# A longer row in the MLP's on-chip tiles: activations 450 instead of 448 columns apart, weights' tiles 898 instead of 896 columns

## The chip, the core and the metric

The kernel runs on one core of a Trainium2 chip. Its engines work side by side, each through its own list of instructions: PE (TensorE, matrix products; its weight loads are shown apart as PEld), DVE (VectorE), ACT (ScalarE), POOL (GpSimd) and SP, which issues most of the DMAs. They meet at semaphores. On-chip memory (SBUF) has 128 partitions, and a tile takes the same byte range in each of them; matrix products land in a second memory, PSUM.

The metric is the time of one execution on the device, in microseconds. Traces come from executions with the hardware profiler on. Times of instructions are in nanoseconds where so marked.

## What is computed

The reference is one block with two residual branches on x of 2048 tokens by 448 channels, each behind a layer norm that is scaled, shifted and gated by a condition vector c. The first branch is a state-space convolution over the tokens, computed in the kernel through hand-made Fourier tables. The second is a small network across the tokens:

```python
x = A_u
mod = (_silu(c) @ w_mod).reshape(c.shape[0], 6, 1, -1)
sa, ca, ga, sb, cb, gb = (mod[:, 0], mod[:, 1], mod[:, 2], mod[:, 3], mod[:, 4], mod[:, 5])
h = _layernorm(x, axis=-1) * (1 + ca) + sa
x = x + ga * _A_ref(h, ...)                      # convolution along the tokens
h = _layernorm(x, axis=-1) * (1 + cb) + sb
x = x + gb * _B_ref(h, B_w1, B_b1, B_w2, B_b2)   # MLP along the tokens

def _B_ref(x, w1, b1, w2, b2):                   # S = 2048 tokens, D = 448, F = 1792
    h = _layernorm(x, axis=-1)                   # (B, S, D)
    u = _gelu(jnp.einsum("bsd,sf->bdf", h, w1) + b1)
    y = jnp.einsum("bdf,fs->bds", u, w2) + b2
    return y.transpose(0, 2, 1)
```

The change touches the tiles of `_B_ref` alone.

## The kernel before

The convolution fills the first 400 us or so. The MLP comes last, and every product of it is made of three matmuls in the type fp32r, a rounded fp32. Each fp32 operand is split into a rounded high part and the remainder as a low part, and the kernel sums high x high, high x low and low x high.

*Activations.* `h3h` and `h3l` (lines 1320 and 1321) hold the high and low part of the normed tokens: 128 partitions, 16 rows of D = 448 columns of four bytes. Row r is the moving operand (`h3h[:, r]`) of the matmuls on lines 1332 to 1334. They are written by ACT (lines 1237 and 1243) and DVE (1240 and 1244), one row for each turn of the loop over t on line 1339. `uh` and `ul` hold the same for the hidden layer after the gelu, in two halves of 7 rows each (lines 1322, 1323, 1387 and 1388). DVE writes them row by row behind ACT's gelu (lines 1373 to 1375), and lines 1401 to 1403 read them.

*Weights.* `WeightStream` brings 64 tiles of 128 x 896. A DMA loads the raw fp32 tile `w` (lines 187 and 190), ACT rounds it into `whi` (line 207), and DVE writes what is left into `wlo` (line 216). `whi` and `wlo` have four buffers each (WAHEAD), `w` three. Each tile has seven slices of 128 columns, and each slice is a stationary operand, loaded into PE ahead of its matmul.

*Loops.* The first layer runs in two halves of seven hidden blocks. For each of the 16 rows r, `mlp1` takes one weight tile and does 7 x 3 matmuls into seven PSUM tiles `acc`. Then comes the gelu of the half. The second layer makes 16 output tiles `o`, each of 2 x 7 x 3 matmuls: kh picks the half of `uh` and `ul`, k the row. In all that is 2 x 16 x 21 + 16 x 42 = 1344 matmuls of 128 x 128 by 128 x 448, 224 on each of the six lines.

*Order.* PE, ACT, DVE and POOL do their work in the order in which the code issues it (`manual_schedule`). Weights are split up to four tiles ahead of use, on ACT and DVE, and a split has to wait until the matmuls have let a buffer go. During the first half, ACT and DVE also make the layer norm's rows (`ln_y`, `ln_mod`, `ln_out`) just ahead of the matmuls that read them. In the second half and the second layer they only split weights, apply the gelu and write outputs (lines 1405 to 1407).

*Other matmuls that the prediction speaks of.* Line 485 makes the modulation vectors in plain fp32: the moving operand is `wm` or, later, rows of `xt`, 448 columns each, and the stationary one is `scb`. Line 1212 belongs to the first two rows of the convolution's output and moves 224 columns against `fl`. Line 1202 makes the other rows.

Of the kernel before, what the change touches and what calls it, by code (L numbers as in the profile page):

```python
# [12 lines left out]
F32R = mybir.dt.float32r  # L13
# [8 lines left out]
L, D, N, F = 2048, 448, 256, 1792  # L22
P = 128
# [136 lines left out]
def token_pair(a, r, g):  # L160

    rows = a.rearrange("(n g h r) d -> g n h (r d)", g=2, h=2, r=16)
    return rows[g, :, :, r * D : (r + 2) * D]


class WeightStream:
# [32 lines left out]
    def begin(self, most):  # L199

        n = self.done
        if n >= min(most, 64):
            return None
        w = self.raw.pop(n)
        hi = self.pool.tile([P, 896], F32R, tag="whi", name="whi")
        lo = self.pool.tile([P, 896], F32R, tag="wlo", name="wlo")
        self.nc.scalar.copy(hi, w)  # L207
        self.parts[n] = hi, lo
        self.done += 1
        return w, hi, lo  # L210
# [11 lines left out]
def tile_adaln_s4d_mixer(ctx, tc, i, out):  # L222
# [20 lines left out]
    with ExitStack() as es:  # L243
# [796 lines left out]
        for s in range(tail):  # L1040
# [80 lines left out]
            if s == 16:  # L1121
                spec.close()
                up = early.enter_context(tc.tile_pool(name="up", bufs=3, reuse_waits="tile"))
# [43 lines left out]
        def ln_load(r, ahead=True):  # L1167
            vts[r] = rot.tile([P, 2, D], F32, tag="vt", name="vt", bufs=4)
            nc.sync.dma_start(vts[r], v_v[r])
            if ahead and r % 2 and 1 < r < 15:  # L1170
                x_pair(r + 1)
# [26 lines left out]
        def ln_y(r):  # L1198
            y = py.tile([P, D], F32, tag="y", name="y")
            vt = vts.pop(r)  # L1200
            for g in range(2):
                T.matmul(y[64 * g : 64 * g + 64], ft, vt[:, g], start=True, stop=True)  # L1202
            return y_sum(r, y)
# [16 lines left out]
        def ln_mod(r):  # L1220
            mean, rs = sa.pop(r)
            h = rot.tile([P, D], F32, tag="h", name="h", bufs=3)
            total = small("sum", "b")
            V.reciprocal(rs, rs)
            V.scalar_tensor_tensor(h, xts[r // 2][:, r % 2], mean, mod[4], ALU.add, ALU.mult)
            V.scalar_tensor_tensor(h, h, rs, mod[3], ALU.mult, ALU.add, accum_out=total)  # L1226
            sb[r] = stats(h, total, "b")
            hs[r] = h

        def ln_out(r):  # L1230
            mean, rs = sb.pop(r)
            h = hs.pop(r)
            V.reciprocal(rs, rs)
            V.tensor_tensor(mean, mean, rs, ALU.mult)
            if r == 0:

                S.activation(h3h[:, r], h, AF.Identity, bias=mean, scale=rs)  # L1237
                exact = rot.tile([P, D], F32, tag="h", name="h", bufs=3)
                V.tensor_scalar(exact, h, rs, mean, ALU.mult, ALU.add)
                V.tensor_tensor(h3l[:, r], exact, h3h[:, r].bitcast(F32), ALU.subtract)  # L1240
                return None
            S.activation(h, h, AF.Identity, bias=mean, scale=rs)  # L1242
            S.copy(h3h[:, r], h)
            return lambda: V.tensor_tensor(h3l[:, r], h, h3h[:, r].bitcast(F32), ALU.subtract)
# [69 lines left out]
    with ExitStack() as es:  # L1314
        es.enter_context(tc.manual_schedule(engines={ENG.PE, ENG.Activation, ENG.DVE, ENG.Pool}))
        V, S, G = nc.vector, nc.scalar, nc.gpsimd
        kp = es.enter_context(tc.tile_pool(name="mk", bufs=1))
        up = es.enter_context(tc.tile_pool(name="mu", bufs=1))
        pacc = es.enter_context(tc.tile_pool(name="pacc", bufs=7, space=PSUM))
        h3h = kp.tile([P, 16, D], F32R, name="h3h")  # L1320
        h3l = kp.tile([P, 16, D], F32R, name="h3l")
        uh = [up.tile([P, 7, D], F32R, name="uh0"), None]
        ul = [up.tile([P, 7, D], F32R, name="ul0"), None]

        def mlp1(acc, n, f0=0, f1=7):
            fh, r = divmod(n, 16)
            hi, lo = wst.parts[n]
            if f1 == 7:
                wst.parts.pop(n)
            for f in range(f0, f1):  # L1330
                fs = slice(f * P, (f + 1) * P)
                nc.tensor.matmul(acc[f], hi[:, fs], h3h[:, r], start=r == 0, stop=False)  # L1332
                nc.tensor.matmul(acc[f], hi[:, fs], h3l[:, r], start=False, stop=False)  # L1333
                nc.tensor.matmul(acc[f], lo[:, fs], h3h[:, r], start=False, stop=r == 15)  # L1334

        first = ExitStack()
        first.enter_context(tc.manual_schedule(engines={ENG.SP}))
        acc = [pacc.tile([P, D], F32, tag="acc", name="acc") for _ in range(7)]
        for t in range(-2, 16):

            part = wst.begin(t + WAHEAD - 1) if t > 0 else None
            last = ln_out(t + 1) if 0 <= t + 1 < 16 else None

            if t == -1:
                second()
            if t == 0:
                part = wst.begin(3)
                mlp1(acc, 0, 0, 4)
                ln_y(3)()
            if t == -1 or 0 < t < 13:  # L1350
                ln_y(t + 3)()
            if 4 <= t + 7 < 16:
                ln_load(t + 7)
            if t < 0:
                wst.load()
            if 1 <= t + 2 < 16:
                ln_mod(t + 2)
            if last:
                last()
            wst.rest(part, V)  # L1360
            if t == 0:
                mlp1(acc, 0, 4, 7)
            elif t > 0:
                mlp1(acc, t)
        first.close()
        e3.close()
        ru = es.enter_context(tc.tile_pool(name="m2r", bufs=3))

        def gelu(acc, fh):
            for f in range(7):  # L1370
                k = 7 * fh + f
                u = ru.tile([P, D], F32, tag="u", name="u")
                S.activation(u, acc[f], AF.Gelu_apprx_tanh, bias=b1[:, k : k + 1])
                V.tensor_copy(uh[fh][:, f], u)
                V.tensor_tensor(ul[fh][:, f], u, uh[fh][:, f].bitcast(F32), ALU.subtract)

        gelu(acc, 0)
        acc = [pacc.tile([P, D], F32, tag="acc", name="acc") for _ in range(7)]
        for r in range(16):
            if r < 8:  # L1380
                for g in range(2):
                    rows = xts[r][64 * g : 64 * g + 64].rearrange("p r d -> p (r d)")
                    nc.sync.dma_start(token_pair(x2_d, 2 * r, g), rows)
            wst.ahead(16 + r + WAHEAD, V)
            mlp1(acc, 16 + r)
        e2.close()
        uh[1] = up.tile([P, 7, D], F32R, name="uh1")
        ul[1] = up.tile([P, 7, D], F32R, name="ul1")
        gelu(acc, 1)
        for t in range(16):  # L1390
            ss = slice(t * P, (t + 1) * P)
            xt = ru.tile([P, D], F32, tag="x2", name="x2")
            nc.sync.dma_start(xt, x2_d[ss])
            o = pacc.tile([P, D], F32, tag="acc", name="o")
            for kh in range(2):
                n = 32 + 2 * t + kh
                wst.ahead(n + WAHEAD, V)
                hi, lo = wst.parts.pop(n)
                for k in range(7):
                    ks = slice(k * P, (k + 1) * P)  # L1400
                    nc.tensor.matmul(o, hi[:, ks], uh[kh][:, k], start=kh == 0 and k == 0, stop=False)  # L1401
                    nc.tensor.matmul(o, hi[:, ks], ul[kh][:, k], start=False, stop=False)  # L1402
                    nc.tensor.matmul(o, lo[:, ks], uh[kh][:, k], start=False, stop=kh == 1 and k == 6)  # L1403
            y = ru.tile([P, D], F32, tag="y", name="y")
            V.scalar_tensor_tensor(y, o, b2[:, t : t + 1], mod[5], ALU.add, ALU.mult)  # L1405
            V.tensor_tensor(y, y, xt, ALU.add)  # L1406
            nc.sync.dma_start(out[0, ss], y)
# [27 lines left out]
```

## Time and profile before

| | us |
|---|---|
| median of three runs | 698.45 (691.95, 698.45, 699.45) |
| profiled execution, its time | 695.37 |
| profiled execution, span from the first to the last instruction | 693.2 |
| PE busy in the span | 621.5 |
| first and last start of a matmul of the MLP | 403.4 and 688.5 |
| mean granted TensorE clock, as a share of full speed | 0.958 |

The prediction shows the lines. A row of a group reads: line, engine, operation, the tiles it writes and reads, how often, then durations. PE and PEld have rows of their own, because a weight load runs beside the matmul before it. The ends of matmuls in the trace are modelled, since they are pipelined; the distance from one start to the next is the better measure of what one costs. An "idle before" belongs to the engine, with the work whose end closed the wait.

### The profile page before, as it was taken

To read this page: it belongs to the slowest core of one execution; us is meant where nothing else is said; L and a number is where in the kernel's file an instruction comes from. 1 tells how busy PE (TensorE), PEld (TensorE's weight loads), DVE (VectorE), ACT (ScalarE), POOL (GpSimd) and SP (SyncE) were. 2 spreads that over 40 slices of the span, in tenths; PEclk is the share of its full clock that TensorE was granted. 3 is DMA by queue.
4 is the path that set the end of the run, shared out by engine and by line. 5 is a ranking of instruction groups with operands and counts; after the bars stand their busy time and mean duration, and the time that the engine had idled before them with its cause. 6 is when DMAs were issued, how large, how long until landed. Compare 5 with 4: busy or idle time off the path is not lost. (4 is left out here: it accounts for less than half of the span.)

```text
span 693.2 us, 18255 instructions
## 1 busy us (share of the span) xinstructions
PE 621.5 (90%) x7180; PEld 462.5 (67%) x7180; DVE 456.7 (66%) x880; ACT 437.6 (63%) x876; POOL 269.2 (39%) x323
## 2 busy tenths in 40 slices
PE   0878889889988779898899989999999999999997
PEld 0444445545535556565567757778999999999996
DVE  7578799879779468685877577776622354444431
ACT  5867599788977789999973578777422332222220
POOL 6497468259368768889766300000000000000000
PEclk9997979899999989899999999999999999999999
DMA  7694646567895526444248799965674445556540
GB/s 173 195 194 110 219 163 217 208 203 233 252 298 170 156 72 159 128 132 146 84 128 261 245 269 264 243 152 149 168 242 112 141 132 160 160 159 170 167 129 27
DMA packets 104275, 121.14 MB, mean 175 GB/s; under 512 B 12858, under 2 KB 92254, under 8 KB 104062
## 3 DMA queue, kind: packets, MB, share of 16 engines
q1 hardware_dynamic: 102830, 113.92, 56.8%
q0 software_dynamic: 1360, 6.06, 4.1%
q8 instruction: 57, 0.93, 0.6%
q14 instruction: 28, 0.23, 0.1%
HBM read 84.59 MB, written 34.87 MB: 172 GB/s over the span
## 5 line engine op out<-in xcount | busy, mean ns | idle before, releaser
L207 ACT CAST whi<-w 128x896 fp32r<-128x896 f32 x64 | 59.7, 938 | 131.7 <-PE o L1402 84.6
L650 POOL TENSOR_TENSOR G<-mag,gs 128x512 f32<-128x512 f32 x56 | 72.3, 1290 | 73.2 <-ACT gs L646 70.7
L216 DVE TENSOR_TENSOR wlo<-w,whi 128x896 fp32r<-128x896 f32 x64 | 68.0, 1086 | 40.3 <-ACT whi L207 31.0
L1332 PE MATMUL acc<-h3h,whi 128*128 128x448 f32 x224 | 83.3, 372 | 1.4 <-ACT h3h L1237 1.4
L681 PEld LDWEIGHTS kg<-E,G 128*32 128x32 f32 x3584 | 59.1, 118 | 36.5 <-issue 16.4
L1334 PE MATMUL acc<-h3h,wlo 128*128 128x448 f32 x224 | 82.0, 366 | 0.0
L1333 PE MATMUL acc<-h3l,whi 128*128 128x448 f32 x224 | 81.6, 364 | 0.2 <-DVE mean L1186 0.2
L1401 PE MATMUL o<-uh,whi 128*128 128x448 f32 x224 | 81.4, 363 | 0.0
L1403 PE MATMUL o<-uh,wlo 128*128 128x448 f32 x224 | 81.2, 363 | 0.0
L1402 PE MATMUL o<-ul,whi 128*128 128x448 f32 x224 | 80.7, 360 | 0.0
L598 PE MATMUL xg<-tab,lph 64*128 64x512 f32 x112 | 67.4, 604 | 11.6 <-DVE E L658 7.2
L681 PE MATMUL kg<-E,G 128*32 128x64 f32 x3584 | 69.4, 233 | 8.9 <-issue 4.1
L598 PE MATMUL xe<-tab,lph 64*128 64x512 f32 x112 | 66.9, 600 | 9.7 <-ACT gs L647 7.0
L651 POOL TENSOR_TENSOR G<-mag,gs 128x512 f32<-128x512 f32 x56 | 71.6, 1278 | 0.0
L1405 DVE SCALAR_TENSOR_TENSOR y<-o,b,mod 128x448 f32<-128x448 f32 x16 | 11.0, 685 | 80.2 <-PE o L1403 80.2
L627 POOL TENSOR_TENSOR m<-mag,w 128x512 f32<-128x512 f32 x56 | 59.7, 1066 | 4.6 <-POOL w L625 0.3
L652 DVE TENSOR_TENSOR E<-m,xe 128x512 f32<-128x512 f32 x56 | 38.0, 679 | 28.4 <-ACT xe L645 24.5
L1332 PEld LDWEIGHTS acc<-h3h,whi 128*128 128x128 f32 x224 | 42.5, 190 | 13.6 <-ACT h L1242 6.3
L598 PE MATMUL xe<-tab,lex 64*128 64x512 f32 x56 | 32.0, 584 | 18.4 <-POOL dsk L472 17.2
L635 ACT ACTIVATE ab<-xe 128x512 f32<-128x512 f32 x56 | 34.0, 607 | 20.4 <-PE xe L598 11.2
L609 ACT ACTIVATE mag<-xe 128x512 f32<-128x512 f32 x56 | 35.7, 637 | 15.1 <-PE xe L598 6.2
L1334 PEld LDWEIGHTS acc<-h3h,wlo 128*128 128x128 f32 x224 | 42.5, 190 | 3.3
(236 smaller groups left out, 1470.3 us busy)
## 6 DMA issues: line engine op xcount, KB each, us to landing
w<-in_B_w_dram SPq DMA_DIRECT2D x64, 224.0 KB
w<-in_B_w_dram SPq DMA_DIRECT2D x32, 448.0 KB
yu_d<-yt SPq DMA_DIRECT2D x16, 448.0 KB
yi<-yu_d SPq DMA_DIRECT2D x16, 448.0 KB
us_d<-uo SPq DMA_DIRECT2D x16, 448.0 KB
u<-us_d SPq DMA_DIRECT2D x32, 224.0 KB
v_d<-vt SPq DMA_DIRECT2D x32, 224.0 KB
vt<-v_d SPq DMA_DIRECT2D x14, 448.0 KB
```

The source lines that it names most:

```text
L207: self.nc.scalar.copy(hi, w)
L216: eng.tensor_tensor(lo, w, hi.bitcast(F32), ALU.subtract)
L598: T.matmul(out[k], lhs[r], rhs[r], start=start, stop=stop)
L650: G.tensor_tensor(Gt[:, 1], mg_, v32(sg), ALU.mult)
L651: G.tensor_tensor(Gt[:, 0], mg_, v32(cg_), ALU.mult)
L681: T.matmul(kgs[g][32 * q : 32 * q + 32, m], Gt[:, c, d], E[:, c, d], start=h == 0 and c == 0 and m == 0, stop=h == 1 and c == 1, skip_grou ...
L1332: nc.tensor.matmul(acc[f], hi[:, fs], h3h[:, r], start=r == 0, stop=False)
L1333: nc.tensor.matmul(acc[f], hi[:, fs], h3l[:, r], start=False, stop=False)
L1334: nc.tensor.matmul(acc[f], lo[:, fs], h3h[:, r], start=False, stop=r == 15)
L1401: nc.tensor.matmul(o, hi[:, ks], uh[kh][:, k], start=kh == 0 and k == 0, stop=False)
L1402: nc.tensor.matmul(o, hi[:, ks], ul[kh][:, k], start=False, stop=False)
L1403: nc.tensor.matmul(o, lo[:, ks], uh[kh][:, k], start=False, stop=kh == 1 and k == 6)
```

## The change

Five tiles get a row of two more columns, and the code goes on with a view that leaves these two columns out. The two columns are written and read by nothing. `h3h`, `h3l`, `uh` and `ul` get W = D + 2 = 450 columns a row, so rows are 1800 bytes apart instead of 1792. `whi` and `wlo`, which have one row to a partition, get 898 columns, 3592 bytes instead of 3584. The raw tile `w`, into which the DMAs write, stays as it is. A line is added at 1320 (`W = D + 2`), so all lines of the MLP behind it stand one further down in the changed kernel: the matmuls are on 1333 to 1335 and 1402 to 1404.

```diff
@@ class WeightStream, begin
-        hi = self.pool.tile([P, 896], F32R, tag="whi", name="whi")
-        lo = self.pool.tile([P, 896], F32R, tag="wlo", name="wlo")
+        hi = self.pool.tile([P, 898], F32R, tag="whi", name="whi")[:, 0:896]
+        lo = self.pool.tile([P, 898], F32R, tag="wlo", name="wlo")[:, 0:896]
         self.nc.scalar.copy(hi, w)
@@ the MLP's tiles
-        h3h = kp.tile([P, 16, D], F32R, name="h3h")
-        h3l = kp.tile([P, 16, D], F32R, name="h3l")
-        uh = [up.tile([P, 7, D], F32R, name="uh0"), None]
-        ul = [up.tile([P, 7, D], F32R, name="ul0"), None]
+        W = D + 2
+        h3h = kp.tile([P, 16, W], F32R, name="h3h")[:, :, 0:D]
+        h3l = kp.tile([P, 16, W], F32R, name="h3l")[:, :, 0:D]
+        uh = [up.tile([P, 7, W], F32R, name="uh0")[:, :, 0:D], None]
+        ul = [up.tile([P, 7, W], F32R, name="ul0")[:, :, 0:D], None]
@@ after the first layer
-        uh[1] = up.tile([P, 7, D], F32R, name="uh1")
-        ul[1] = up.tile([P, 7, D], F32R, name="ul1")
+        uh[1] = up.tile([P, 7, W], F32R, name="uh1")[:, :, 0:D]
+        ul[1] = up.tile([P, 7, W], F32R, name="ul1")[:, :, 0:D]
```

In the allocation of the built programs, `h3h` begins at byte 22304 of each partition in both kernels, and all six activation tiles begin 32 bytes past a multiple of 64. The weights' buffers were 3584 bytes apart, and are now 3616.

## The prediction

> **What bounds the kernel now.** I read the profile's page first (busy shares and chain), then busy time by stretch from the start of the MLP on, then the six matmul groups of the MLP with the smallest, middle and largest duration, then the timeline inside one stretch, and last what TensorE waited for.
>
> The profile's page has the span, the engines and the chain that ended last:
>
> ```profile
> span 693.2 us, 18255 instructions
> PE 621.5 (90%) x7180; PEld 462.5 (67%) x7180; DVE 456.7 (66%) x880; ACT 437.6 (63%) x876; POOL 269.2 (39%) x323
> ...
> PE acc L1332 7%; PE o L1401 7%; PE acc L1334 7%; PE acc L1333 7%; PE o L1403 6%; PE o L1402 6%; PE y L1202 2%; ACT whi L207 0%; ACT sq L1188 0%; ACT L1291 0%; ACT h3h L1237 0%; DVE h L1226 0%; DVE y L1405 0%; DVE h3l L1240 0%; DVE y L1406 0%
> ```
>
> All of the chain that the profile names at 6% and more is matmuls of the MLP, the instructions that read the tiles of the change. The stretches of the MLP, with busy time of PE, PEld, DVE, ACT, POOL, then clock, DMA share and GB/s:
>
> ```profile
> 420.00:440.00 20.00, 20.00 (x95) 15.08 (x94) 15.06 (x46) 16.32 (x36) 0.00 (x0) 1.00 1.06 259
> 440.00:460.00 20.00, 20.00 (x96) 15.08 (x95) 15.03 (x44) 15.99 (x35) 0.00 (x0) 1.00 0.95 213
> ...
> 480.00:554.00 74.00, 74.00 (x372) 69.39 (x371) 28.06 (x38) 23.38 (x30) 0.00 (x0) 1.00 0.60 171
> 554.00:693.20 139.20, 134.89 (x675) 126.14 (x673) 55.33 (x71) 29.67 (x33) 0.00 (x0) 1.00 0.48 138
> ```
>
> From 420 on PE has no idle time up to the last matmul. What PE waited for in the whole MLP (from 403 us) is two short waits at its start, 1.6 us together:
>
> ```profile
> PE acc L1332 <- ACT h3h L1237: 1.4, 1, 1.4
> PE acc L1333 <- DVE mean L1186: 0.2, 1, 0.2
> ```
>
> So the time from 403 us on is the number of MLP matmuls times their spacing. The groups that write `acc` and `o` (smallest, middle, largest duration in ns, then first and last start in us):
>
> ```profile
> L1332 PE MATMUL acc<-h3h,whi x224: 362/363/575, 403.4 to 553.7; 128*128 128x448 f32 x112
> L1333 PE MATMUL acc<-h3l,whi x224: 359/360/739, 404.1 to 553.9; 128*128 128x448 f32 x112
> L1334 PE MATMUL acc<-h3h,wlo x224: 360/363/576, 404.6 to 554.1; 128*128 128x448 f32 x112
> ...
> L1401 PEld LDWEIGHTS o<-uh,whi x224: 187/188/188, 554.1 to 687.9; 128*128 128x128 f32 x112
> L1401 PE MATMUL o<-uh,whi x224: 363/363/364, 554.3 to 688.1; 128*128 128x448 f32 x112
> ...
> L1402 PE MATMUL o<-ul,whi x224: 359/360/361, 554.5 to 688.3; 128*128 128x448 f32 x112
> ...
> L1403 PE MATMUL o<-uh,wlo x224: 362/363/368, 554.7 to 688.5; 128*128 128x448 f32 x112
> ```
>
> The 672 matmuls of the second half start from 554.3 to 688.5: 134.2 / 671 = 200.0 ns each. The timeline shows the same rhythm and the weight load beside it:
>
> ```profile
> 560.12 0.36 PE L1403 MATMUL o<-uh,wlo 128*128 128x448 f32 x1
> 560.12 0.19 PEld L1401 LDWEIGHTS o<-uh,whi 128*128 128x128 f32 x1
> 560.32 0.36 PE L1401 MATMUL o<-uh,whi 128*128 128x448 f32 x1
> 560.32 0.19 PEld L1402 LDWEIGHTS o<-ul,whi 128*128 128x128 f32 x1
> 560.52 0.36 PE L1402 MATMUL o<-ul,whi 128*128 128x448 f32 x1
> ```
>
> A load starts with the matmul before it, lasts 187 to 188 ns and ends 12 ns ahead of the next start. It is hidden; the 200 ns are the reading of 448 columns of a `h3h`, `h3l`, `uh` or `ul` row. All 1344 together are 1344 x 0.2 = 268.8 us of the 693.2. 1% of the time is 7.0 us, or 5.2 ns per MLP matmul, and about that much a measurement of this kernel can tell from no change.
>
> **The change, part by part.** The built program has the same instructions in the same order with the same waits, DMA issues included; only addresses differ. So no term comes from an added or moved instruction or a new wait, and each has to come from an instruction that lasts longer or shorter at its new place. In the allocation of the built programs `h3h` starts at byte 22304 of a partition, 32 past a multiple of 64, and `h3l`, `uh` and `ul` also stand at 32. Before, rows are 1792 bytes apart, a multiple of 64, and each row begins at 32 modulo 64. After, they are 1800 bytes apart and row r begins at 32 + 8r modulo 64.
>
> *Counts.* In the first half 14 of 16 rows leave the place 32, in the second 6 of 7: 672 x 14/16 + 672 x 6/7 = 588 + 576 = 1164 matmuls. Off every multiple of 32 are 12 of 16 and 5 of 7: 504 + 480 = 984. At 8 modulo 16 are 8 of 16 and 3 of 7: 336 + 288 = 624.
>
> *Moving operand (the only term on the path).* The trace of before has no matmul that reads a row at 8, 16 or 24 past a multiple of 32, so its price is bounded by the nearest rows. These are the plain fp32 matmuls, which stand as two records for each matmul of the program. L485 reads rows at 32 (`wm`) and rows at 0 modulo 64 (`xt`), and L1212 reads 224 columns at 32:
>
> ```profile
> L485 PEld LDWEIGHTS pm<-wm,scb x24: 186/190/337, 39.5 to 82.8; 112*128 112x128 f32 x24
> L485 PE MATMUL pm<-wm,scb x24: 538/539/1116, 39.5 to 83.2; 112*128 112x448 f32 x24
> ...
> L485 PE MATMUL pm<-xt,scb x24: 539/539/644, 109.8 to 146.9; 112*128 112x448 f32 x24
> L1212 PEld LDWEIGHTS y<-vt,fl x32: 186/190/191, 389.7 to 398.8; 128*128 128x128 f32 x32
> L1212 PE MATMUL y<-vt,fl x32: 352/353/458, 389.7 to 399.0; 128*128 128x224 f32 x32
> ```
>
> 539 against 539 ns: at those two places there is no difference. But they take (539 - 353) / 224 = 0.83 ns a column, and leave 353 - 224 x 0.83 = 167 ns that doesn't depend on columns. The MLP's fp32r matmul takes (363 - 167) / 448 = 0.44 ns a column, so it reads a row at about twice the rate, and may feel what L485 doesn't. At half of 0.83 it would last 353 ns; it lasts 363 with `h3h` or `uh` and 360 with `h3l` or `ul`, on average 9 ns more. These 9 ns are the only excess in the rows that a place could cause. Lower end: a row that leaves 32 loses all of it, 1164 x 9 = 10.5 us less. Upper end: a row off the multiples of 32 pays it once more, 984 x 9 = 8.9 us more. I take 0, from L485, whose pair of rows is the only like-for-like comparison of places.
>
> The Trainium skill (SBUF — State Buffer, Specifications) says that SBUF lines are 16 bytes and that each crossing to a new line pays a penalty, which speaks against this change. A row at 8 modulo 16 touches 113 such lines instead of 112; at an estimate of 1/112 of the 200 ns for the extra one, 624 matmuls would add 1.1 us, so by the rule the sum would be +1.1 us and by L485's rows 0. No row of before reads at such a place, so the trace can't decide between them, and both lie under what can be measured.
>
> *Weight loads.* `whi` and `wlo` tiles of 3592 bytes lie 3616 apart in their pool, so the tiles start at 32, 0, 32, 0 modulo 64, not at all places, and each slice of 128 columns keeps its tile's place. L485 loads `scb` at 0 and L1212 loads `fl` at 32: 190 ns both. Taken as 0; cover is the 12 ns ahead of the next matmul, and a load that grew by more would put the excess on the path of 1344 matmuls (5 ns over the cover is 6.7 us).
>
> *ACT and DVE.* The rows that write these tiles, over the MLP (count, busy us, mean ns, idle before and its releaser):
>
> ```profile
> L216 DVE TENSOR_TENSOR wlo<-w,whi 128x896 fp32r<-128x896 f32 x62 | 65.8, 1085 | 39.6 <-ACT whi L207 30.2 <-DMA w<-in_B_w_dram 9.3
> L207 ACT CAST whi<-w 128x896 fp32r<-128x896 f32 x62 | 57.9, 938 | 131.7 <-PE o L1402 84.6 <-PE acc L1333 38.5 <-DMA w<-in_B_w_dram 8.7
> ...
> L1375 DVE TENSOR_TENSOR ul<-u,uh 128x448 fp32r<-128x448 f32 x14 | 8.7, 625 | 0.5
> ...
> L1374 DVE CAST uh<-u 128x448 fp32r<-128x448 f32 x14 | 5.4, 387 | 6.0 <-ACT u L1373 6.0
> ```
>
> L207 mostly waits for PE to free a buffer: splits run ahead and are hidden as long as L216 stays under the 21 matmuls of a weight tile, 4.2 us, against 1.09. The one row that could lose a faster mode is L1374, which copies 448 columns in 387 ns where L1375 takes 625. If it fell to 625, the seven copies of a half would end 7 x 0.24 = 1.7 us later. Cover: the last `ul` of the second half starts at 557.8 and ends at 558.4, and PE wants that row with the 41st matmul of the half at 554.3 + 40 x 0.2 = 562.3, so 3.9 us are free. If the cover were gone, PE would be late at the first L1401 of kh = 1, once. In the first half (420 to 480) DVE is busy 15 and ACT 16 of 20 us, so a few per cent on `h3h` and `h3l` fit too. Cost 0.
>
> *Sum.* 0 on the profiled execution's 693.2 us of span and 695.4 us of time. The median of the runs is 698.45, 3.1 us above the profiled one; the runs reach from 691.95 to 699.45. Forecast: 698.5.
>
> **The rivals.**
> 1. Slower: the fp32r read of a row off the multiples of 32 pays as much again as the excess. Place: L1332 to L1334 and L1401 to L1403, all on the path. Price 9 ns x 984 = 8.9 us, 707.3. For it: the read is at twice the rate of the row that shows no difference, and no place of this sort has been tried in the trace. Against it: nothing in the rows shows a read that depends on place. It decides from 7.0 us / 984 = 7.1 ns.
> 2. Faster: the 9 ns come from beginning at 32 modulo 64, and rows elsewhere lose them. 1164 x 9 = 10.5 us, 688.0. For it: all MLP rows stand at 32 and all have the excess. Against it: it has to vanish at seven different places at once, and `h3l` has 3 ns less than `h3h` at the same place, so place isn't all of it.
> 3. The change does nothing to what bounds: weights' tiles begin at two places only and their loads are hidden, and the rows' places don't matter. That is the forecast's own time, 698.5.
>
> **How the numbers follow.** Within 1%: 0.74, for the equal durations of L485, the unchanged order and the cover of loads and splits. Slower by over 1%: 0.16, rival 1 and whatever puts a weight load over its 12 ns. Faster by over 1%: 0.10, rival 2. The forecast's own range is the spread of the runs, 691.9 to 699.5. To leave out no more than 2 in 10 the range takes rival 1 up to 707 and goes down to 690.5, which is part of rival 2.
>
> **What would show it.** In the changed profile the second half's matmuls still start 200 ns apart and last 360 to 364 ns, and within the seven rows of a turn the durations don't differ. Rival 1 would show as middle durations of 370 and more in five of seven rows, rival 2 as 353. A weight load that matters would last over 200 ns. L1374's copy at 387 or 625 ns tells about DVE; PE waiting at the first matmul of kh = 1 would say its cover was too small. I am wrong if spacing changes by over 5 ns, or if PE idles between 420 and 688 us.

## The result and the profile after

The changed kernel takes 701.36 us (median of 18 runs) against 694.76 us for the kernel before on the same chip (18 runs). The ratio is 1.0088, 95% interval 1.0065 to 1.0111: slower by 0.9%, about 6.1 us. That is inside the forecast's range and inside its class of changes within 1% (the interval reaches a little beyond), but it is clear of noise, and the forecast's own figure was no change.

The page of the profiled execution after, span, engines and chain:

```profile
span 697.1 us, 18255 instructions
PE 625.8 (90%) x7180; PEld 463.7 (67%) x7180; DVE 456.0 (65%) x880; ACT 438.7 (63%) x876; POOL 269.8 (39%) x323
...
PE acc L1333 7%; PE acc L1334 7%; PE acc L1335 7%; PE o L1403 7%; PE o L1404 7%; PE o L1402 7%; PE y L1202 2%; ACT whi L207 0%; ACT sq L1188 0%; ACT L1291 0%; ACT h3h L1237 0%; DVE h L1226 0%; DVE y L1406 0%; DVE y L1407 0%; ACT rs L1189 0%
```

The same instructions bound the kernel. Busy time by stretch (us of PE, PEld, DVE, ACT, POOL, then clock, DMA share, GB/s), first a stretch that is nearly all in the second half of the first layer, then the second layer from its first to its last start:

```profile
480.00:554.00 74.00, 74.00 (x364) 68.30 (x363) 26.55 (x35) 22.19 (x27) 0.00 (x0) 1.00 0.59 170
555.50:692.40 136.90, 136.90 (x673) 126.38 (x672) 53.73 (x69) 29.43 (x33) 0.00 (x0) 1.00 0.49 138
```

PE is busy without a gap at the full granted clock, as before. But 74 us now hold 364 matmuls where they held 372, and the second layer, with the same 672 matmuls, starts its last one 136.7 us behind its first where it took 134.2. The groups of the second layer (smallest, middle, largest duration in ns, first and last start in us):

```profile
L1402 PEld LDWEIGHTS o<-uh,whi x224: 187/188/191, 555.5 to 691.8; 128*128 128x128 f32 x112
L1402 PE MATMUL o<-uh,whi x224: 359/366/370, 555.7 to 692.0; 128*128 128x448 f32 x112
...
L1403 PE MATMUL o<-ul,whi x224: 358/366/373, 555.9 to 692.2; 128*128 128x448 f32 x112
...
L1404 PE MATMUL o<-uh,wlo x224: 362/365/373, 556.1 to 692.4; 128*128 128x448 f32 x112
```

(692.4 - 555.7) / 671 = 203.7 ns from start to start (203.8 from the unrounded starts), 200.0 before. The middle duration went from 363 or 360 to 366, and what was a spread of 1, 2 and 6 ns on the three lines became one of 11 to 15. Weight loads still last 187 to 188 ns. In the timeline the regular 0.20 becomes a mixture of 0.20 and 0.21:

```profile
500.20 0.37 PE L1334 MATMUL acc<-h3l,whi 128*128 128x448 f32 x1
500.40 0.37 PE L1335 MATMUL acc<-h3h,wlo 128*128 128x448 f32 x1
500.61 0.37 PE L1333 MATMUL acc<-h3h,whi 128*128 128x448 f32 x1
500.81 0.36 PE L1334 MATMUL acc<-h3l,whi 128*128 128x448 f32 x1
501.01 0.36 PE L1335 MATMUL acc<-h3h,wlo 128*128 128x448 f32 x1
```

PE's only listed wait in the MLP is at its start, 1.6 us as before:

```profile
PE acc L1333 <- ACT h3h L1237: 1.6, 1, 1.6
```

And ACT and DVE write the tiles at their new places as fast as they did at the old ones (938, 1085, 625 and 387 ns before):

```profile
L216 DVE TENSOR_TENSOR wlo<-w,whi 128x896 fp32r<-128x896 f32 x62 | 65.9, 1086 | 40.7 <-ACT whi L207 31.1 <-DMA w<-in_B_w_dram 9.6
L207 ACT CAST whi<-w 128x896 fp32r<-128x896 f32 x62 | 57.9, 938 | 134.9 <-PE o L1403 87.2 <-PE acc L1334 39.7 <-DMA w<-in_B_w_dram 8.0
...
L1376 DVE TENSOR_TENSOR ul<-u,uh 128x448 fp32r<-128x448 f32 x14 | 8.8, 626 | 0.5
L1375 DVE CAST uh<-u 128x448 fp32r<-128x448 f32 x14 | 5.4, 388 | 6.5 <-ACT u L1374 6.5
```

From the first to the last start of a matmul the MLP takes 285.1 us before (403.4 to 688.5) and 291.1 after (401.3 to 692.4), 6.0 us more. 1344 x 3.8 ns = 5.1 us of it is spacing. The other 0.9 us lies in the first few matmuls of the MLP, where the kernel after has one gap of 2.0 us from start to start, for 1.2 before, and a low granted clock for a little longer (0.56 from 405 to 408 us, for 0.96 from 407 to 410 before); a single execution can't say whether that belongs to the change.

Neither figure is 1344 times the spacing, which would be 268.8 us before. In the first half of the first layer PE also does the plain fp32 matmuls of line 1202, the sums that the layer norm's rows start from. They stand in 13 gaps of 1.2 us between matmuls of the MLP, the same before and after but for the one of 2.0 us. Its rows before and after (count, busy us, mean ns, idle before):

```profile
L1202 PE MATMUL y<-vt,ft 128*64 128x448 f32 x52 | 12.6, 565 | 0.0
```

```profile
L1202 PE MATMUL y<-vt,ft 128*64 128x448 f32 x52 | 13.3, 590 | 0.0
```

So the question is what makes a matmul of the same size stream 3.8 ns longer. Three theories went into the experiments. **Row**: each matmul pays for the place of its own moving row. **Weights**: the weights' tiles that begin at 0 modulo 64 cost. **Pair**: what counts is the distance in bytes from the weight slice that is being loaded to the row that is being read during that load. In the kernel before, rows start at 32 and weight slices at 224 modulo 256, so each row is at distance 32 - 224 = 64 modulo 256 from each slice, always.

### The profile page after: what moved, and what is told of

The parts are those of the page before. It is cut to its first block, busy times and chain, and to the rows that moved or that the text cites. A ratio compares the mean times of both kernels' runs of the same rounds, so it can differ in the third digit from the quotient of the medians.

```text
span 697.1 us, 18255 instructions
## 1 busy us (share of the span) xinstructions
PE 625.8 (90%) x7180; PEld 463.7 (67%) x7180; DVE 456.0 (65%) x880; ACT 438.7 (63%) x876; POOL 269.8 (39%) x323
## 5 line engine op out<-in xcount | busy, mean ns | idle before, releaser
L681 PE MATMUL kg<-E,G 128*32 128x64 f32 x3584 | 70.8, 236 | 7.2 <-issue 3.4
L1334 PEld LDWEIGHTS acc<-h3l,whi 128*128 128x128 f32 x224 | 42.7, 191 | 3.7 <-DVE h3l L1240 0.4
```

The lines of the kernel that those rows point to most:

```text
L681: T.matmul(kgs[g][32 * q : 32 * q + 32, m], Gt[:, c, d], E[:, c, d], start=h == 0 and c == 0 and m == 0, stop=h == 1 and c == 1, skip_grou ...
```

## The experiments

In all of them the instructions and their order are those of the kernel before, except in the two with half loads. Spacings below are means of the differences between start times in the trace, over the second half of the first layer and over the second layer; the granted clock there is 1.00 in every run. A turn is the 21 matmuls of one weight tile. Places are those of the built programs' allocation. `f3_lowscan`, `f4_half`, `f5_pitch464`, `f6_half_e4` and `f7_highscan` have one execution each, so for them only spacings are told.

**Half of the change each.** The change widens six named tiles, not five: `h3h`, `h3l`, `uh` and `ul`, and `whi` and `wlo`. `e1_rows` is the change without its two lines on the weights, `e2_weights` those two lines alone.

```diff
# e1_rows
+        W = 450
-        h3h = kp.tile([P, 16, D], F32R, name="h3h")
+        h3h = kp.tile([P, 16, W], F32R, name="h3h")[:, :, 0:D]
...
# e2_weights
-        hi = self.pool.tile([P, 896], F32R, tag="whi", name="whi")
+        hi = self.pool.tile([P, 898], F32R, tag="whi", name="whi")[:, 0:896]
...
```

> Only the activations' rows are 450 columns apart; weights' tiles keep 896 columns and all stand at 32 modulo 64 (224 modulo 256). In the changed kernel the MLP matmuls start 203.8 ns apart on average (200.0 before). Row theory (a matmul pays for the place of its own moving row, whatever the weights do): 203.8 ns here too, +5 us, and the spacing of a row is the same wherever it has the same place modulo 64. Pair theory (what counts is the place of the moving row against that of the weight slice that is loaded during the same matmul): spacing between 200 and 206 ns, other than 203.8, and a row's spacing depends on more than its place modulo 64. Weights theory (the tiles at 0 modulo 64 cost): 200.0 ns and no change of time.

> Only the weights' tiles have 898 columns, so they begin at 32 and 0 modulo 64 in turn; all activation rows stay at 32 modulo 64. Row theory: 200.0 ns and no change of time. Pair theory: a spacing that differs from 200.0 by 1 ns or more in some of the four buffers, and by buffer. Weights theory: 203.8 ns, +5 us.

Measured: `e1_rows` 203.6 ns in the first layer and 204.1 in the second, ratio 1.0103 (1.0065 to 1.0141). `e2_weights` 202.7 ns in both, ratio 1.0067 (1.0033 to 1.0100). Either half alone makes the kernel slower, and the two together (203.8) are no slower than the rows alone, so they aren't two costs that add. In `e2_weights` no row has moved. The second layer:

```profile
L1401 PE MATMUL o<-uh,whi x224: 362/366/368, 552.5 to 688.1; 128*128 128x448 f32 x112
L1402 PE MATMUL o<-ul,whi x224: 360/366/370, 552.7 to 688.3; 128*128 128x448 f32 x112
L1403 PE MATMUL o<-uh,wlo x224: 358/364/369, 552.9 to 688.5; 128*128 128x448 f32 x112
```

(688.5 - 552.5) / 671 = 202.7. Sorted by the four buffers that a weight tile can stand in, with the distance modulo 256 from the `whi` and the `wlo` slice to the row:

```
distance to whi / wlo    mean spacing of the buffer's 21 matmuls, every turn
 64 / 192                200.1 ns
  0 / 128                202.4
 32 / 160                203.6
224 /  96                204.6
```

The figures come back in each turn within 0.1 ns. In `e1_rows` rows 0 and 8 of the first layer both begin at 32 modulo 64 and take 200.2 and 202.1 ns. The row theory, by which these two are equal and `e2_weights` is unchanged, falls; so does the weights theory, by which `e1_rows` is unchanged.

**Same spacing of rows, another beginning.** Rows stay 448 columns apart and each tile begins 2 or 8 columns later, which makes all rows alike again.

```diff
+        def packed(pool, n, name, off):
+            flat = pool.tile([P, n * D + 64], F32R, name=name)
+            return flat[:, off : off + n * D].rearrange("p (r d) -> p r d", d=D)
-        h3h = kp.tile([P, 16, D], F32R, name="h3h")
+        h3h = packed(kp, 16, "h3h", 8)     # e3_shift8: 2, f2_rows32 and f1_both: 56
...
```

> Rows stay 448 columns apart, but each activation tile begins two columns later, so that every row stands at 40 modulo 64; weights as before. Row theory: the spacing that rows at 40 have in the changed kernel, 205.3 ns on average, everywhere, +7 us. Pair theory: one uniform pattern of three spacings, whose mean is not that 205.3 ns, because the weights stand elsewhere than in the changed kernel; it may be under 200. Weights theory: 200.0 ns.

> Rows stay 448 columns apart, each activation tile begins eight columns later, so that every row stands at 0 modulo 64; weights as before. Row theory: the spacing of rows at 0 in the changed kernel, 203.7 ns on average, +5 us; a form of it by which a row at a whole multiple of 64 reads one piece less gives 193 ns, -9 us. Pair theory: one uniform pattern, its mean anywhere from 196 to 206 ns. Weights theory: 200.0 ns.

Measured: `e3_shift8` (distance 72) 206.5 ns in the first layer and 205.1 in the second, ratio 1.0113 (1.0051 to 1.0175). `e4_shift32` (distance 96) 205.3 ns in both, ratio 1.0104 (1.0047 to 1.0161). `e4_shift32` has every row at a whole multiple of 64 bytes (at 64 modulo 256) and is slower than the changed kernel's mixture, so a row that begins in the middle of 64 bytes is not the trouble, and the hoped-for 193 ns is out. `e3_shift8` alone would roughly have fitted the row theory (205.3). But its second layer isn't the one uniform pattern that was expected of the pair theory: although every distance is 72, the seven rows of a half take 202.4 to 206.9 ns, nearly the same in both halves. At 72, then, the distance modulo 256 isn't all that counts.

**The decisive four.** With rows at 0 modulo 256 and weights where they were, the distance is 32 (`f2_rows32`). With both 32 bytes lower it is 64 again (`f1_both`; its rows begin 224 bytes later, which is 32 less modulo 256). With the weights alone 32 bytes lower it is 96 (`g1_weights32`), as in `e4_shift32`, where the rows had moved instead. The weights move by a small tile that is put last into their pool; the raw `w` tiles move along.

```diff
+        if n == 0:
+            self.pool.tile([P, 8], F32, tag="pad", name="pad", bufs=1)
         self.nc.scalar.copy(hi, w)
```

> Activation rows and weights' tiles both stand 32 bytes lower than before (rows at 0 modulo 64 and 128, weights at 192 modulo 256), so every row keeps its distance to every weight slice modulo 128: 64, as before. e4_shift32 has its rows at 0 modulo 64 too and takes 205.3 ns. Pair theory (the distance of row and weight slice modulo 128 decides): 200.0 ns, in the pattern 201, 197, 202, and no change of time within 0.5%. Row theory (the row's own place decides): 205.3 ns and +7 us.

> Rows at 0 modulo 64 and 128 as in f1_both, weights where they were before: distance 32 modulo 128. Pair theory: what the buffer of e2_weights at distance 32 shows, 203.6 ns, +4.8 us. Row theory: the same as in e4_shift32 and f1_both, 205.3 ns.

> The activation rows stay where they were before; only the weights' tiles stand 32 bytes lower (at 192 modulo 256, as in f1_both). The distance of rows to weights becomes 96 modulo 256, as in e4_shift32, where instead the rows had moved. Pair theory: the 205.3 ns of e4_shift32, in its pattern of five, and +7 us, though no row has moved. Any theory by which row and weights each pay for their own place: rows at their place of before cost nothing, and weights at 192 cost nothing in f1_both, so 200.0 ns and no change.

The second layer of `e4_shift32`, `f1_both`, `f2_rows32` and `g1_weights32`, in this order:

```profile
L1405 PE MATMUL o<-uh,whi x224: 365/367/370, 558.1 to 695.5; 128*128 128x448 f32 x112
L1406 PE MATMUL o<-ul,whi x224: 365/367/370, 558.3 to 695.7; 128*128 128x448 f32 x112
L1407 PE MATMUL o<-uh,wlo x224: 365/367/370, 558.5 to 695.9; 128*128 128x448 f32 x112
```

```profile
L1407 PE MATMUL o<-uh,whi x224: 362/363/363, 550.4 to 684.2; 128*128 128x448 f32 x112
L1408 PE MATMUL o<-ul,whi x224: 362/364/364, 550.7 to 684.5; 128*128 128x448 f32 x112
L1409 PE MATMUL o<-uh,wlo x224: 359/360/361, 550.9 to 684.7; 128*128 128x448 f32 x112
```

```profile
L1405 PE MATMUL o<-uh,whi x224: 368/370/370, 554.7 to 692.9; 128*128 128x448 f32 x112
...
L1407 PE MATMUL o<-uh,wlo x224: 367/370/370, 555.1 to 693.4; 128*128 128x448 f32 x112
```

```profile
L1403 PE MATMUL o<-uh,whi x224: 365/367/370, 555.8 to 693.2; 128*128 128x448 f32 x112
L1404 PE MATMUL o<-ul,whi x224: 365/367/370, 556.0 to 693.4; 128*128 128x448 f32 x112
L1405 PE MATMUL o<-uh,wlo x224: 365/367/370, 556.2 to 693.6; 128*128 128x448 f32 x112
```

The first and the last are alike to the nanosecond, and the second has the durations of the kernel before again, though it shares no place with it. Fifteen spacings in a row from the second layer, in ns:

```
                rows  weights  distance   start to start                                                mean
before            32      224        64   201 196 203 201 197 201 202 197 202 200 198 202 201 197 202   200.0
f1_both            0      192        64   202 200 198 202 200 198 202 200 198 202 201 198 201 200 198   200.0
e4_shift32        64      224        96   205 207 204 203 208 205 207 204 202 209 205 206 204 203 208   205.3
g1_weights32      32      192        96   205 207 204 203 208 205 207 204 202 209 205 206 205 202 208   205.3
f2_rows32          0      224        32   207 207 206 207 207 206 207 207 206 207 208 205 207 207 206   206.7
```

`f1_both` has the ratio 0.9992 (0.9961 to 1.0023), `f2_rows32` 1.0126 (1.0086 to 1.0167) and `g1_weights32` 1.0077 (1.0034 to 1.0119). Two pairs of kernels share no place, only the distance, and have the same spacing; three kernels with all rows at 0 modulo 64 (`f1_both`, `e4_shift32`, `f2_rows32`) have three different ones. Rows moved from 32 to 0 modulo 256 cost 6.7 ns with the weights at 224 (`f2_rows32` against before) and gain 5.3 with the weights at 192 (`f1_both` against `g1_weights32`), so no sum of a price for the row's place and one for the weights' place can give these four. That the distance decides, at the 32, 64 and 96 bytes of these five kernels, is thereby shown. The size that was expected for `f2_rows32`, 203.6 from the buffer at 32 / 160, was wrong: with both slices at 32 it is 206.7. The writes of ACT and DVE into the tiles aren't behind it: in `g1_weights32` the spacing is 205.3 ns beside a busy DVE and beside an idle one, and within 0.1 ns the same for ACT.

What these runs don't separate is the slice that is being loaded from the slice that the matmul is using, since in each of them all slices stand alike modulo 256. One hint is in `e2_weights`: in the buffer at 64 / 192 the third matmul of each three takes 202 ns, but 204 at the end of the tile, where the slice loaded beside it is the next buffer's.

**Is it the amount that is loaded?** If reading the slice and reading the row got in each other's way, half a slice should hurt less. The second and third matmul of each three take 64 columns of weights, and so make 64 rows of output instead of 128:

```diff
-                    nc.tensor.matmul(o, hi[:, ks], ul[kh][:, k], start=False, stop=False)
-                    nc.tensor.matmul(o, lo[:, ks], uh[kh][:, k], start=False, stop=kh == 1 and k == 6)
+                    nc.tensor.matmul(o[0:64], hi[:, ks][:, 0:64], ul[kh][:, k], start=False, stop=False)
+                    m = P if kh == 1 and k == 6 else 64
+                    nc.tensor.matmul(o[0:m], lo[:, ks][:, 0:m], uh[kh][:, k], start=False, stop=kh == 1 and k == 6)
...
```

> All places as before (distance 64), but the second and third matmul of each three use 64 of the 128 columns of their weight slice, but for the last third matmul of a PSUM tile; half of the output rows of these two products is left out. The moving rows that are read stay the same. Shared-read theory (the weight load's reading and the row's reading get in each other's way): a matmul beside which only half as much is loaded streams faster, so the mean falls clearly under 200 ns, to 192 to 197. Row theory, or a fixed cost from one matmul to the next: 200.0 ns still.

> The same half loads with the places of e4_shift32 (distance 96), which takes 205.3 ns with full loads, 5.3 more than at distance 64; again half of the output rows of two of the three products is left out. Shared-read theory: two of three loads read half as much, so the difference to f4_half is smaller, 1.5 to 4 ns, and both are under their kernels with full loads. Row theory: 205.3 ns, 5.3 ns over f4_half.

`f4_half`, second layer:

```profile
L1403 PEld LDWEIGHTS o<-ul,whi x224: 133/134/136, 550.9 to 685.6; 128*64 128x64 f32 x112
L1403 PE MATMUL o<-ul,whi x224: 360/362/370, 551.1 to 685.8; 128*64 128x448 f32 x112
...
L1405 PE MATMUL o<-uh,wlo x224: 358/363/368, 551.3 to 686.0; 128*64 128x448 f32 x112
```

The loads shrink from 187 to 134 ns, but the spacing is 201.4 ns, not the 192 to 197 that the theory of shared reading gave. It is even 1.4 ns longer than with full loads. `f6_half_e4` has 204.4 ns, 0.9 less than with full loads and 3.0 more than `f4_half` instead of 5.3, which lies in the expected band. So halving the load doesn't shorten the spacing at distance 64, and the plain theory of shared reading falls by its main figure. The distance still matters with half loads, though less.

**The period, the pitch, and a better place.** In `f5_pitch464` all rows are 464 columns apart. `f3_lowscan` gives the longer row of 450 columns to `h3l` and `ul` alone, `f7_highscan` to `h3h` and `uh` alone.

```diff
# f5_pitch464
+        W = 464
-        h3h = kp.tile([P, 16, D], F32R, name="h3h")
+        h3h = kp.tile([P, 16, W], F32R, name="h3h")[:, :, 0:D]
...
# f3_lowscan
-        h3l = kp.tile([P, 16, D], F32R, name="h3l")
+        h3l = kp.tile([P, 16, D + 2], F32R, name="h3l")[:, :, 0:D]
...
# f7_highscan
-        h3h = kp.tile([P, 16, D], F32R, name="h3h")
+        h3h = kp.tile([P, 16, D + 2], F32R, name="h3h")[:, :, 0:D]
...
```

> Activation rows 464 columns (1856 bytes) apart, weights as before: rows alternate between distance 64 and 0 modulo 128 from the weights. Pair theory: rows at distance 64 keep 200.0 ns although the pitch is longer than in the changed kernel, rows at distance 0 take the 202.4 ns that e2_weights has there; 201.2 ns on average. Were it the longer pitch as such, all rows would take more than 203 ns.

> Only h3l and ul have rows 450 columns apart; h3h, uh and the weights keep distance 64. So only the second matmul of each three reads at a new distance, 64 + 8r modulo 128. Pair theory: 200.0 ns in row 0 of the first layer, and in the other rows between 200 and 205, less where the distance is a multiple of 16 bytes (in e1_rows such rows average 202.7 ns and the others 204.5). If any row falls clearly under 200 ns, there is a place that beats the kernel before.

> The reverse: only h3h and uh have rows 450 columns apart, so the first and third matmul of each three read at distance 64 + 8r, the second at 64 modulo 128. Pair theory: row 0 at 200.0 ns, the others between 200 and 206, nearer to e1_rows than f3_lowscan is, and again less at multiples of 16 bytes. A row clearly under 200 ns would be a better place.

In `f5_pitch464` the rows of the first layer stand at distances 64, 128, 192 and 0 modulo 256, one after the other, and take 200.5, 204.0, 202.1 and 202.6 ns, each time. The row at 64 nearly keeps its 200 although the pitch is longer, so the pitch as such costs no more than 0.5 ns. But 192 isn't 64, so the period is not the 128 bytes I had assumed, and the layer's 202.3 ns is more than the 201.2 expected. 256 agrees with the kernel before, where the rows lie 7 x 256 bytes and the slices 2 x 256 bytes apart and all behave alike. The second layer, 203.5 ns on average, goes further against the plain rule: there `uh` and `ul` begin at different places, and rows with the same two distances, `uh` at 128 and `ul` at 64, take 204.1 and 204.2 ns in one half and 200.6 in the other. So where distances are mixed, the distances modulo 256 don't fix a row's spacing. In `f3_lowscan` row 0 takes 200.6 ns and the others 201.9 to 204.5; in `f7_highscan` row 0 takes 200.2, row 6 200.0 and the others 202.6 to 206.5. The finer order that `e1_rows` had suggested (202.7 ns on average at distances that are multiples of 16 bytes, 204.6 at the others) isn't in `f3_lowscan`, where the distances 8 and 0 modulo 128 take 201.9 and 204.3. No row of the first layer falls clearly under 200 ns. In `f7_highscan`'s second layer two of the seven rows of one half have 197.5 and 198.1 ns, next to rows at 202 to 204, and that layer as a whole has 202.2. There `uh` is at distance 16 and 24 and `ul` at 64. By the expectation's own words these are better places, for two rows in that surrounding; no run put all rows there, and no version came out that beats the kernel before.

## Why the forecast held, and where its working failed

- *What bounds the kernel* was right: the spacing of 1344 matmuls, with no gap on PE and with the loads ahead. Most of the effect, 5.1 us of 6.0, could be found in that one figure. But "the time from 403 us on is the number of MLP matmuls times their spacing" left out line 1202 and the first, slow matmuls: 268.8 us against 285.1. As both kernels have them, the forecast didn't suffer.
- *The moving operand, taken as 0 from L485*: this step failed. The term measured 3.8 ns a matmul, 5.1 us. Two rows with equal durations had stood for all places. But L485 reads at half the rate, by the prediction's own sum, and its two rows stand at distances 32 (`wm`) and 128 (`xt`) modulo 256 from `scb`: the distance 64, which the MLP had and lost, isn't in the comparison. Whether the rate or the distances made it blind, no run shows. Places were also counted modulo 64 only, where all activation tiles begin alike. Modulo 256 the changed kernel's `h3h` and `h3l` begin at 32 and 160, and its eight weight buffers at eight different places.
- *The range* held by luck. Its bounds come from an excess of 9 ns that the rows' place doesn't explain (`f1_both` moves the rows and keeps it), and happened to be wide enough for 3.8 ns on all 1344 matmuls. The figure 698.5 came within 2.9 us of 701.36 only because its base, the median of three executions, was 3.7 us above the 694.76 of the 18; the miss of the change itself is 6.1 us.
- *Rival 1* had the right sign and, at 8.9 us for 6.1, a size too large by half, with a wrong mechanism. It put the price on rows off the multiples of 32. Rows that all stand at multiples of 32 take 205.3 or 206.7 ns.
- *Rival 2*, the excess comes from beginning at 32 modulo 64: refuted by `f1_both`, which begins elsewhere and has the same durations and the same 200.0 ns.
- *Rival 3*, the weights' places do nothing: refuted by `e2_weights` and `g1_weights32`. The prediction asked whether a load lasts longer, and it doesn't. It never asked whether a matmul lasts longer beside a load from another place.
- *ACT and DVE* at no cost: right, every duration is the same within 2 ns.
- *The line rule of the Trainium skill* (SBUF — State Buffer, Specifications (TRN2)), with its estimate of 1.1 us for rows at 8 modulo 16: too small for what was measured, and it doesn't tell the cases apart, since the rows that take 205.3 and 206.7 ns begin at whole lines.
- *What would show it*: the test named there, durations that don't differ among the seven rows of a turn, is the one that caught the error. The other sign, a spacing that changes by over 5 ns, let the 3.8 ns pass.

The Trainium skill (TensorE: Matmul & The Clock Gate, Step-by-step: what each phase is for) says that loading the next tile's weights takes no read bandwidth from the running matmul. The halved loads agree with that as far as bandwidth goes: at 201.4 ns they brought no shorter spacing. But moving nothing except the weights' buffers took it from 200.0 to 205.3.

What stays open is the mechanism behind the distance: why 64 is good and 96 or 32 isn't, what besides the distance modulo 256 counts at 72 bytes and in mixtures, and which slice matters, the one in use or the one being loaded. The traces show when instructions start, not what a read waits for.

## What to carry to other kernels

Where a long run of matmuls is the whole chain, take the start-to-start time of the matmuls first, and compare it with the place of the moving row against the place of the weight slices, since padding either one changes it. Of the four uniform distances tried here (32, 64, 72 and 96), the best has a spacing 3% shorter than the worst (200.0 against 206.7 ns), with the same instructions. An equal duration in another group is evidence only if that group reads at the same rate and covers the places that the change leaves and enters.

## What the runs showed that was not expected

- A change of 32 bytes in where the weights' buffers stand, with every instruction the same, costs 0.8% of the kernel (`g1_weights32`).
- The short spacing of each three isn't tied to an operand. Before, it is the second matmul's (197 of 201, 197, 202); in `f1_both` it is the third's, and in `e4_shift32` the pattern repeats after five matmuls though the program repeats after three. So it isn't the data or the tile that makes one of them short.
- In three of the spacings one step recurs: 200.0 is 30 x 6.667 ns, 206.7 is 31 x 6.667, and five spacings of `e4_shift32`, 5 x 205.33 = 1026.7 ns, are 154 x 6.667. `e3_shift8`, with 206.5 and 205.1 ns, doesn't show it. This is arithmetic on the means; no run here shows what the step is, or that there is one.
